# Attention and a two-layer network on one core: bursts of three chunks, A@V and three chunks, and another load of the first quad

## The chip, the cores and the metric

The kernel runs on one core of a Trainium2 chip. A core has five engines that run side by side, each through its own list of instructions in order: TensorE (PE in the profile, with PEld for the loading of weights), VectorE (DVE), ScalarE (ACT), GpSimd (POOL) and SyncE (SP). Semaphores order them against each other. TensorE reads on-chip memory (SBUF) and writes to PSUM, eight banks of 512 f32 values in each of 128 partitions; VectorE and ScalarE empty PSUM. Transfers between HBM and SBUF are issued from SP, ACT or POOL.

The metric is the device time of one execution in microseconds. Before the change it is 388.61 us, the median of three runs (388.48 to 388.9).

## The reference

Eight batches of 12 heads, 448 tokens, 64 dimensions per head. Each head's attention is a squared ReLU in place of a softmax, and its result feeds a network with 2048 hidden values:

```
scores = q @ k.T / sqrt(64)
attn   = max(scores, 0) ** 2 / 448
x      = attn @ v                       # heads side by side: 3584 tokens x 768
h      = x @ w_in                       # 768 -> 2048
g      = max(h, 0) + alpha * min(h, 0)
out    = g @ w_out                      # 2048 -> 768, float32
```

## The kernel before

Four heads of a batch make a *quad*; there are three quads per batch, 24 in all, numbered `n`. The 448 tokens are 64 times 7; a *chunk* `j` of 0 to 6 is one seventh of k's tokens for the four heads of a quad. So a quad has seven chunks.

Per quad there are these steps. **Loads**: `load_qk` and `load_v` bring q, k and v by POOL's queue, casting f32 to bf16 on the way. **Turning**: q and k are needed with the head dimension on partitions (tile `T`). For quads 0 to 5 `turn_pe` does it by transposes on PE (L153) and copies out of PSUM on DVE or ACT (L156); for later quads `turn_dma` has DVE rearrange them (L161) and SP issue a transposing DMA (L163). **Scores**: `score_mm` (L175) is one chunk, four matmuls of 64 x 64 weights on the four quarters of the array, which run side by side, into a pair of PSUM banks. **ReLU**: L184 on ACT or L186 on DVE, out of PSUM. **Square**: L194 on DVE or L192 on ACT. **A@V**: `attnv` (L204), 28 matmuls on quarters of the array, seven steps of four, into a pair of banks; the first bank is emptied by ACT (L214) and the second by DVE (L215) into `xT`.

Per batch there are then two stages that use the whole array. `f1` (L238) makes one of 16 blocks of 128 hidden values with six matmuls, and `f1_out` forms the leaky ReLU with ACT (L246) and DVE (L247) into `gT`. `f2` (L261) makes a block of 128 tokens by 384 output columns with 16 matmuls over `gT`; the copy out of PSUM is on ACT (L263) and two DMAs on SP write it (L269). Since `gT` covers two batches, six such blocks come behind an even batch and eight behind an odd one.

The order is written out by hand: the scheduler is off (`manual_schedule`), so every engine runs in the order of the program's lines. The attention of the next batch is laid between the blocks of the present one. In the loop over batches 2 to 7 the unit is `burst(n)`: three chunks of scores, A@V of quad n, two chunks, then all squares that are due. A *plain burst*, `run(some(3))`, is three chunks and their squares alone. Per batch there are two plain bursts, ahead of f1 blocks 6 and 12, and three bursts between output blocks, two output blocks apart (three in places). `prepare(n)` turns quad n by DMA and issues the loads of quad n + 2; it stands ahead of f1 blocks 1 and 9 and ahead of the second burst. Batches 0 and 1 are written out in single lines, since their attention has to be made before there is other work to lay it between.

PSUM is handed out in turn: `take_bank` gives the bank that was taken longest ago and `take_pair` the pair whose later bank was taken longest ago. Whoever gets a bank waits until what was in it has been read.

At the start q of quad 0 comes in f32 by SP's queue and the first four of its seven blocks of k by ACT's queue, both plain; DVE and ACT cast them. The last three blocks of k come by POOL's casting queue (L129). Transposes of those three stand behind three chunks of scores. 36 matmuls of an identity (L133) run meanwhile. POOL's queue goes on with q and k of quad 1, v of quad 0, q and k of quad 2, v of quads 1 and 2, and then the weights.

Of the kernel before, what the change touches and what calls it, by code (L numbers as in the profile page):

```python
# [10 lines left out]
F32 = mybir.dt.float32  # L11
BF16 = mybir.dt.bfloat16
# [4 lines left out]
NJ = 7  # L17
# [3 lines left out]
def kernel(  # L21
# [18 lines left out]
    HALF = d_model // 2  # L40
# [16 lines left out]
    ident = singles.tile([128, 128], BF16)  # L57
# [26 lines left out]
    def take_bank():  # L84
        i = min(range(8), key=lambda i: (taken[i], i))
        take(i, 1)
        return psum[:, i]


    raw, vraw = {}, {}  # L90

    def load_qk(n):
        b, g = divmod(n, NG)
        for name, src in (("q", q), ("k", k)):
            t = raw_pool.tile([128, 2, NJ, D], BF16, tag=name, name=f"{name}raw")
# [21 lines left out]
    def load_w_out(h):  # L117
        nc.gpsimd.dma_start(out=w_out_sb[:, h], in_=w_out_v[h])

    FIRST = 4  # L120
    first, flat0 = {}, {}
    for name, src, eng, hi in (("q", q, nc.sync, NJ), ("k", k, nc.scalar, FIRST)):
        first[name] = singles.tile([128, 2, hi * D], F32, name=f"{name}first")
        flat0[name] = src[0].rearrange("(m two) (pp j) d -> (two pp) m (j d)", two=2, j=NJ)[:, :2]
        eng.dma_start(out=first[name], in_=flat0[name][:, :, :hi * D])
        raw[(0, name)] = raw_pool.tile([128, 2, NJ, D], BF16, tag=name, name=f"{name}raw")
    nc.sync.dma_start(out=alpha_sb, in_=moe_alpha.rearrange("(kf p) -> p kf", p=128))
    make_identity(nc, ident)
    nc.gpsimd.dma_start(out=raw[(0, "k")][:, :, FIRST:].rearrange("p m j d -> p m (j d)"),  # L129
                        in_=flat0["k"][:, :, FIRST * D:])  # L130
    warm = psum[:, 7, :128]
    for _ in range(36):
        nc.tensor.matmul(warm, ident, ident, start=True, stop=True)  # L133
    for name, lo, hi, copy in (("q", 0, 4, nc.vector.tensor_copy), ("q", 4, NJ, nc.scalar.copy),
                               ("k", 0, 2, nc.vector.tensor_copy), ("k", 2, FIRST, nc.scalar.copy)):
        copy(raw[(0, name)][:, :, lo:hi].rearrange("p m j d -> p m (j d)"), first[name][:, :, D * lo:D * hi])  # L136
    load_qk(1)
    load_v(0)
    load_qk(2)
    load_v(1)  # L140
    load_v(2)


    T = {}

    def turn_pe(n, parts=(("q", 0, NJ, "D"), ("k", 0, NJ, "D"))):
        if n not in T:
            T[n] = T_pool.tile([128, 2, NJ, 128], BF16, tag="T", name="T")
        for name, lo, hi, eng in parts:
            ps = take_bank().bitcast(BF16)  # L150
            for j in range(lo, hi):
                for s in range(2):
                    nc.tensor.transpose(ps[64 * s:64 * s + 64, 128 * j:128 * j + 128], raw[(n, name)][:, s, j], ident)  # L153
            dst = T[n][:, "qk".index(name), lo:hi].rearrange("p j c -> p (j c)")
            copy = nc.vector.tensor_copy if eng == "D" else nc.scalar.copy
            copy(dst, ps[:, 128 * lo:128 * hi])  # L156

    def turn_dma(n):
        p = perm_pool.tile([128, 2, NJ, 2, D], BF16, tag="perm", name="perm")
# [21 lines left out]
    def relu(ps, eng):  # L181
        rl = rl_pool.tile([128, 2, S], BF16, tag="rl", name="rl")
        if eng == "A":
            nc.scalar.activation(rl, ps[:, :, :S], ACTF.Relu)  # L184
        else:
            nc.vector.tensor_scalar(rl, ps[:, :, :S], 0.0, None, ALU.max)  # L186
        return rl
# [31 lines left out]
    def sc(chunks):  # L219

        for n, j, eng in chunks:
            late.append((n, j, relu(score_mm(n, j), eng)))

    def sq(k=99, eng="D"):
        for g in late[:k]:
            square(*g, eng)
        del late[:k]

    def run(chunks):
        sc(chunks)  # L230
        sq()
# [21 lines left out]
        f1_mm(ps, b, ff, range(KM))  # L253
        f1_out(ps, b, ff)

    def f2(sb, c, hf, parts=((0, HALF),)):
        o = o_pool.tile([128, HALF], F32, tag="o", name="osb")
        for lo, hi in parts:
            ps = take_bank()[:, :hi - lo]
            for ff in range(KF):  # L260
                nc.tensor.matmul(ps, gT[sb][:, ff, bass.ts(c, 128)], w_out_sb[:, hf, ff, lo:hi],  # L261
                                 start=(ff == 0), stop=(ff == KF - 1))
            nc.scalar.copy(o[:, lo:hi], ps)  # L263
            for u in range(2):
                blk = 2 * c + u
                b, j = 2 * sb + blk // NJ, blk % NJ
                rows = out[b * S:(b + 1) * S].rearrange("(pp j) d -> j pp d", j=NJ)
                eng = nc.scalar if u and hi - lo < HALF else nc.sync
                eng.dma_start(out=rows[j][:, hf * HALF + lo:hf * HALF + hi], in_=o[64 * u:64 * u + 64, lo:hi])  # L269


    pat = "ADAAAAA"
# [1 line left out]
    def ch(n, lo, hi, p=pat):  # L274
        return [(n, j, p[j]) for j in range(lo, hi)]

    load_w_in(0)
    load_w_in(1)
    turn_pe(0, (("q", 0, 4, "D"), ("q", 4, NJ, "A"), ("k", 0, 2, "D"), ("k", 2, FIRST, "D")))
    sc(ch(0, 0, 3))  # L280
    turn_pe(0, (("k", FIRST, NJ, "D"),))
    sc(ch(0, 3, 4))
    sq(3)
    load_qk(3)
    sc(ch(0, 4, 6))
# [70 lines left out]
    f1s(0, 8, 9)  # L356
    ps = take_bank()[:, :S]
    f1_mm(ps, 0, 9, range(KM))
    turn_pe(4, (("q", 0, NJ, "A"), ("k", 0, NJ, "D")))
    f1_out(ps, 0, 9)  # L360
    load_qk(7)
    load_v(7)
    f1s(0, 10, 12)
    sc(ch(3, 6, 7) + ch(4, 0, 2, "AA"))
    f1s(0, 12, 16)
    f2(0, 0, 0)
    sc(ch(4, 2, 5, "AAADAAA"))
    attnv(3)
    sc(ch(4, 5, 7, "AAAAAAD"))
    turn_pe(5)  # L370
    sq(3)
    sq(2, "A")
    load_qk(8)
    load_v(8)
    f2(0, 1, 0)
    sc(ch(5, 0, 3))
    attnv(4)
    sc(ch(5, 3, 5, "AAAADAA"))
    sq(3)
    sq(2, "A")  # L380
    f2(0, 2, 0)
    sc(ch(5, 5, 7, "AAAAAAD"))
    sq(1, "A")
    sq(1)


    chunks = [(n, j) for n in range(2 * NG, NQ) for j in range(NJ)]
# [2 lines left out]
    def some(k):  # L390
        lo = at_c[0]
        at_c[0] = min(lo + k, len(chunks))
        return [(n, j, e) for (n, j), e in zip(chunks[lo:at_c[0]], "ADA")]

    def burst(n):

        sc(some(3))
        attnv(n)
        sc(some(2))
        sq()  # L400

    early = []
    for ff in range(4):
        ps = take_bank()[:, :S]
        f1_mm(ps, 1, ff, range(4))
        early.append(ps)
        if ff == 1:
            attnv(5)
    for ff in range(KF):
        if ff < 4:  # L410
# [15 lines left out]
    f2(0, 1, 1)  # L426
    run(some(3))
    f2(0, 2, 1)
    run(some(3))
    f2(0, 4, 0)  # L430
    burst(6)
    f2(0, 4, 1)
    f2(0, 5, 0)
    prepare(10)
    burst(7)
    f2(0, 5, 1)
    f2(0, 6, 0)
# [59 lines left out]
```

## Time and profile before

| What | Value |
|---|---|
| Time, median of three runs | 388.61 us |
| Time of the profiled execution | 388.61 us |
| Its span, first to last instruction | 386.8 us |
| PE busy | 377.8 us, 98% of the span |
| DVE, ACT, POOL busy | 69%, 53%, 17% |
| f2 matmuls (L261) | 912, 151.1 us |
| f1 matmuls (L238) | 768, 149.5 us |
| scores (L175) | 672, 45.5 us |
| A@V (L204) | 672, 37.6 us |
| Granted clock of PE | 1.00 |

Matmuls are pipelined, and the matmuls on quarters of the array run side by side, so busy time of PE is no measure of how well it is used; the start times of successive blocks are. A line of the timeline gives the start and the length in us, the engine, the line of the kernel, the operation, output and inputs, the number of instructions merged into the line, and, in brackets, how long the engine stood idle before and what ended that. A line of the chain gives shares of the span by the engine whose work, or whose wait, the end of the program hangs on.

### The profile page before, as it was taken

What the parts mean: (1) busy time and instruction counts of PE and PEld (TensorE: products, weight loads), DVE (VectorE), ACT (ScalarE), POOL (GpSimd) and SP (SyncE); (2) the same over time, 40 slices, a digit from 0 to 9 for tenths busy, and PEclk for the clock granted to TensorE, in tenths of its full rate; (3) what the DMA queues carried; (4) which work ended last, traced back from release to release, by engine and by line L of the source; (5) the groups of instructions that cost most, each with busy time, mean ns of one, the idle gap of its engine ahead of it and who ended that gap; (6) DMA issues with size and microseconds to landing.
All of it is one profiled execution on the core that took longest, in us unless ns stands there. A gap on an engine that the chain in (4) does not pass through costs nothing.

```text
span 386.8 us, 7918 instructions
## 1 busy us (share of the span) xinstructions
PE 377.8 (98%) x3228; PEld 211.1 (55%) x3228; DVE 266.0 (69%) x421; ACT 206.4 (53%) x332; POOL 64.0 (17%) x95
## 2 busy tenths in 40 slices
PE   7799999999999999999999999999999999999996
PEld 5444564555665456545555455654555545655564
DVE  4977876786868878789655896689754887626300
ACT  5977686355555664455445554547543475434311
POOL 8567211421022202022110221120000000000000
PEclk9999999999999999999999999999999999999999
DMA  9999999999393775687292871937025300120023
GB/s 163 187 204 204 204 213 216 157 188 197 79 151 73 115 134 82 122 140 114 47 175 51 138 120 42 176 53 140 22 68 99 74 0 23 42 61 2 14 70 82
DMA packets 71365, 42.97 MB, mean 111 GB/s; under 512 B 38432, under 2 KB 71328, under 8 KB 71328
## 3 DMA queue, kind: packets, MB, share of 16 engines
q0 software_dynamic: 26768, 22.45, 39.8%
q1 hardware_dynamic: 44128, 19.65, 24.0%
q8 instruction: 25, 0.41, 0.4%
q10 hardware_dynamic: 432, 0.36, 0.3%
q14 instruction: 12, 0.10, 0.1%
HBM read 45.62 MB, written 11.01 MB: 146 GB/s over the span
## 4 chain that ended last, share of the span: by engine, by line
PE 94%; DVE 3%; DMA 1%; ACT 1%; issue 0%; ACTq 0%
PE psum L238 38%; PE psum L261 38%; PE psum L175 9%; PE psum L204 8%; DMA qfirst<-in_q_dram 1%; DVE at L194 1%; PE psum L153 1%; DVE T L156 1%; ACT rl L184 1%; DVE rl L186 1%; ACT osb L263 0%; ACTq L269 0%; DVE qraw L136 0%; ACTq L184 0%; ACTq L263 0%
## 5 line engine op out<-in xcount | busy, mean ns | idle before, releaser
L261 PE MATMUL psum<-w_out_sb,gT 128*128 128x384 bf16 (+2 forms) x912 | 151.1, 323 | 0.0
L238 PE MATMUL psum<-xT,w_in_sb 128*128 128x448 bf16 x768 | 149.5, 353 | 0.4 <-ACT rl L184 0.4
L261 PEld LDWEIGHTS <-gT 128*128 128x128 bf16 x912 | 86.7, 98 | 63.0 <-issue 8.2
L238 PEld LDWEIGHTS <-w_in_sb 128*128 128x128 bf16 x768 | 73.7, 98 | 72.4 <-issue 5.6
L247 DVE SCALAR_TENSOR_TENSOR gT<-neg,beta_sb,psum 128x448 bf16<-128x448 f32 x128 | 83.2, 676 | 30.7 <-ACT neg L246 30.7
L246 ACT ACTIVATE neg<-psum 128x448 f32<-128x448 f32 x128 | 69.3, 547 | 64.0 <-PE psum L238 59.7
L184 ACT ACTIVATE rl<-psum 128x896 bf16<-128x896 f32 x112 | 97.2, 933 | 0.5 <-PE psum L175 0.5
L194 DVE TENSOR_TENSOR at<-rl 128x896 bf16<-128x896 bf16 x162 | 90.6, 616 | 0.0
L186 DVE TENSOR_SCALAR rl<-psum 128x896 bf16<-128x896 f32 x56 | 60.8, 1086 | 43.1 <-PE psum L175 43.1
L263 ACT COPY osb<-psum 128x384 f32<-128x384 f32 (+2 forms) x57 | 27.0, 474 | 105.3 <-PE psum L261 98.4
L175 PE MATMUL psum<-T 64*64 64x448 bf16 x672 | 45.5, 356 | 2.9 <-DVE T L156 1.4
L97 POOL DMA_DIRECT2D qraw<-in_q_dram x23 | 16.5, 718 | 172.0 <-DVE perm L161 162.8
L204 PE MATMUL psum<-at,vraw 64*64 64x448 bf16 x672 | 37.6, 351 | 0.3 <-DVE at L194 0.2
L204 PEld LDWEIGHTS <-vraw 64*64 64x64 bf16 x672 | 24.3, 106 | 11.0 <-issue 2.8
L175 PEld LDWEIGHTS <-T 64*64 64x64 bf16 x672 | 18.2, 105 | 21.5 <-issue 14.4
L215 DVE TENSOR_SCALAR xT<-psum 128x448 bf16<-128x448 f32 x23 | 14.4, 624 | 16.1 <-PE psum L204 11.7
L97 POOL DMA_DIRECT2D kraw<-in_k_dram x23 | 16.5, 717 | 14.0 <-DMA w_out_sb<-in_moe_w_out_dram 12.9
L104 POOL DMA_DIRECT2D vraw<-in_v_dram x24 | 17.2, 718 | 0.8 <-issue 0.3
L214 ACT ACTIVATE xT<-psum 128x448 bf16<-128x448 f32 x23 | 12.7, 551 | 3.2 <-PE psum L204 3.2
L161 DVE COPY perm<-qraw 128x896 bf16<-128x896 bf16 x18 | 11.0, 611 | 2.6 <-DMA T<-perm 2.6
L114 POOL DMA_DIRECT2D w_in_sb<-in_moe_w_in_dram x16 | 10.1, 629 | 7.6 <-DMA w_in_sb<-in_moe_w_in_dram 3.0
L161 DVE COPY perm<-kraw 128x896 bf16<-128x896 bf16 x18 | 10.9, 608 | 0.0
(24 smaller groups left out, 41.3 us busy)
## 6 DMA issues: line engine op xcount, KB each, us to landing
out_dram<-osb SPq DMA_DIRECT2D x110, 96.0 KB, 2.2
vraw<-in_v_dram POOLq DMA_DIRECT2D x24, 224.0 KB, 7.7
qraw<-in_q_dram POOLq DMA_DIRECT2D x23, 224.0 KB, 4.9
kraw<-in_k_dram POOLq DMA_DIRECT2D x23, 224.0 KB, 6.6
w_in_sb<-in_moe_w_in_dram POOLq DMA_DIRECT2D x16, 192.0 KB, 8.0
w_out_sb<-in_moe_w_out_dram POOLq DMA_DIRECT2D x2, 1536.0 KB, 18.6
qfirst<-in_q_dram SPq DMA_DIRECT2D x1, 448.0 KB, 4.3
T<-perm SPq DMA_TRANSPOSE x18, 6.9
```

The source lines that it names most:

```text
L97: nc.gpsimd.dma_start(out=t.rearrange("p m j d -> p m (j d)"), in_=flat[:, 2 * g:2 * g + 2])
L161: nc.vector.tensor_copy(p[:, i], raw.pop((n, name)).rearrange("p s j d -> p j s d"))
L175: nc.tensor.matmul(ps[64 * c:64 * c + 64, r, :S], t[64 * r:64 * r + 64, 1, j, 64 * c:64 * c + 64], t[64 * r:64 * r + 64, 0, :, 64 * c:64 * ...
L184: nc.scalar.activation(rl, ps[:, :, :S], ACTF.Relu)
L186: nc.vector.tensor_scalar(rl, ps[:, :, :S], 0.0, None, ALU.max)
L194: nc.vector.tensor_tensor(a, rl, rl, ALU.mult)
L204: nc.tensor.matmul(ps[64 * s:64 * s + 64, r, :S], vv[64 * r:64 * r + 64, s, j, :], a[64 * r:64 * r + 64, s], start=(j == 0), stop=(j == NJ ...
L238: nc.tensor.matmul(ps, w_in_sb[:, km // 2, km % 2, bass.ts(ff, 128)], xT[b][:, km // 2, km % 2, :], start=(km == 0), stop=(km == KM - 1))
L246: nc.scalar.activation(neg, ps, ACTF.Relu, scale=-1.0)
L247: nc.vector.scalar_tensor_tensor(gT[b // 2][:, ff, (b % 2) * S:(b % 2) * S + S], neg, beta_sb[:, ff:ff + 1], ps, ALU.mult, ALU.add)
L261: nc.tensor.matmul(ps, gT[sb][:, ff, bass.ts(c, 128)], w_out_sb[:, hf, ff, lo:hi], start=(ff == 0), stop=(ff == KF - 1))
L263: nc.scalar.copy(o[:, lo:hi], ps)
```

## The change

Six things change.

1. `burst(n)` has three chunks behind A@V in place of two, and squares five of its six chunks on DVE and one on ACT.
2. Per batch one plain burst is left, ahead of f1 block 6. The three `prepare` calls stand ahead of f1 blocks 1, 8 and 13, and none ahead of a burst (but for quad 10, whose place ahead of an output block is kept).
3. The copy of the last output block ahead of a burst is made by DVE in place of ACT (`eng="D"`).
4. In the last third of batch 0 and at the start of batch 1 the bursts are cut anew: the turn of quad 5 comes ahead of A@V 3, with one of its copies on ACT; the burst around A@V 3 has three chunks behind it (the last two of quad 4 and the first of quad 5), the one around A@V 4 has the other six of quad 5, so the burst of two chunks goes; two output blocks follow each other; A@V 5 comes one f1 block later.
5. Ahead of the first large burst there are three plain bursts in place of four.
6. At the start q and k of quad 0 both come whole in f32 by SP's and ACT's queues. DVE casts four blocks of q; ACT casts the other three and all of k. All transposes of quad 0 stand ahead of its first scores, and all four copies out of PSUM are DVE's. POOL's queue begins with v of quad 0, and then has q, k and v of quads 1 and 2.

```diff
-    FIRST = 4
-    first, flat0 = {}, {}
-    for name, src, eng, hi in (("q", q, nc.sync, NJ), ("k", k, nc.scalar, FIRST)):
...
+    first = {}
+    for name, src, eng in (("q", q, nc.sync), ("k", k, nc.scalar)):
+        first[name] = singles.tile([128, 2, NJ * D], F32, name=f"{name}first")
+        eng.dma_start(out=first[name], in_=src[0].rearrange("(m two) (pp j) d -> (two pp) m (j d)", two=2, j=NJ)[:, :2])
...
-    nc.gpsimd.dma_start(out=raw[(0, "k")][:, :, FIRST:].rearrange("p m j d -> p m (j d)"),
-                        in_=flat0["k"][:, :, FIRST * D:])
+    load_v(0)
...
-    for name, lo, hi, copy in (("q", 0, 4, nc.vector.tensor_copy), ("q", 4, NJ, nc.scalar.copy),
-                               ("k", 0, 2, nc.vector.tensor_copy), ("k", 2, FIRST, nc.scalar.copy)):
-        copy(raw[(0, name)][:, :, lo:hi].rearrange("p m j d -> p m (j d)"), first[name][:, :, D * lo:D * hi])
-    load_qk(1)
-    load_v(0)
-    load_qk(2)
-    load_v(1)
-    load_v(2)
+    for name, cut in (("q", ((0, 4, nc.vector.tensor_copy), (4, NJ, nc.scalar.copy))),
+                      ("k", ((0, 2, nc.scalar.copy), (2, NJ, nc.scalar.copy)))):
+        t = raw_pool.tile([128, 2, NJ, D], BF16, tag=name, name=f"{name}raw")
+        for lo, hi, copy in cut:
+            copy(t[:, :, lo:hi].rearrange("p m j d -> p m (j d)"), first[name][:, :, D * lo:D * hi])
+        raw[(0, name)] = t
+    for n in range(1, NG):
+        load_qk(n)
+        load_v(n)
...
-    def f2(sb, c, hf, parts=((0, HALF),)):
+    def f2(sb, c, hf, parts=((0, HALF),), eng="A"):
...
-            nc.scalar.copy(o[:, lo:hi], ps)
+            (nc.vector.tensor_copy if eng == "D" else nc.scalar.copy)(o[:, lo:hi], ps)
...
-    turn_pe(0, (("q", 0, 4, "D"), ("q", 4, NJ, "A"), ("k", 0, 2, "D"), ("k", 2, FIRST, "D")))
-    sc(ch(0, 0, 3))
-    turn_pe(0, (("k", FIRST, NJ, "D"),))
-    sc(ch(0, 3, 4))
+    turn_pe(0, ((0, 4, "D"), (4, NJ, "D")), ((0, 2, "D"), (2, NJ, "D")))
+    sc(ch(0, 0, 4))
     sq(3)
...
-    f2(0, 0, 0)
+    f2(0, 0, 0, eng="D")
+    turn_pe(5, ((0, NJ, "A"),))
     sc(ch(4, 2, 5, "AAADAAA"))
     attnv(3)
-    sc(ch(4, 5, 7, "AAAAAAD"))
-    turn_pe(5)
+    sc(ch(4, 5, 7, "AAAAAAD") + ch(5, 0, 1))
     sq(3)
-    sq(2, "A")
+    sq(1, "A")
+    sq()
     load_qk(8)
     load_v(8)
     f2(0, 1, 0)
-    sc(ch(5, 0, 3))
+    f2(0, 2, 0, eng="D")
+    sc(ch(5, 1, 4, "AADAAAA"))
     attnv(4)
-    sc(ch(5, 3, 5, "AAAADAA"))
+    sc(ch(5, 4, 7, "AAAAADA"))
     sq(3)
-    sq(2, "A")
-    f2(0, 2, 0)
-    sc(ch(5, 5, 7, "AAAAAAD"))
     sq(1, "A")
     sq(1)
+    sq(1, "A")
...
         sc(some(3))
         attnv(n)
-        sc(some(2))
-        sq()
+        sc(some(3))
+        sq(5)
+        sq(1, "A")
...
-        if ff == 1:
+        if ff == 2:
             attnv(5)
...
     f2(0, 2, 1)
-    run(some(3))
-    f2(0, 4, 0)
+    f2(0, 4, 0, eng="D")
     burst(6)
     f2(0, 4, 1)
-    f2(0, 5, 0)
     prepare(10)
+    f2(0, 5, 0, eng="D")
     burst(7)
     f2(0, 5, 1)
-    f2(0, 6, 0)
+    f2(0, 6, 0, eng="D")
     burst(8)
...
-            if not last and ff in (6, 12):
+            if not last and ff == 6:
                 run(some(3))
-            if not last and ff in (1, 9):
-                prepare(n0 + 2 + ff // 8)
+            if not last and ff in (1, 8, 13):
+                prepare(n0 + 2 + (1, 8, 13).index(ff))
...
-                g = at[i]
-                if g == 1:
-                    prepare(n0 + 4)
-                burst(n0 + g)
+                burst(n0 + at[i])
...
-                f2(*u)
+                f2(*u, eng="D" if i + 1 in at and not last else "A")
```

The function `turn_pe` is rewritten to take the cuts of q and of k apart; what it issues for a quad is 28 transposes and the copies out of PSUM, as before.

More of the change, by code (lines that the diff above doesn't have):

```diff
@@ L118, in load_w_out @@
         nc.gpsimd.dma_start(out=w_out_sb[:, h], in_=w_out_v[h])
-    FIRST = 4
-    first, flat0 = {}, {}
-    for name, src, eng, hi in (("q", q, nc.sync, NJ), ("k", k, nc.scalar, FIRST)):
[L123 to L126, printed above, removed]
+    first = {}
+    for name, src, eng in (("q", q, nc.sync), ("k", k, nc.scalar)):
+        first[name] = singles.tile([128, 2, NJ * D], F32, name=f"{name}first")
+        eng.dma_start(out=first[name], in_=src[0].rearrange("(m two) (pp j) d -> (two pp) m (j d)", two=2, j=NJ)[:, :2])
     nc.sync.dma_start(out=alpha_sb, in_=moe_alpha.rearrange("(kf p) -> p kf", p=128))
     make_identity(nc, ident)
-    nc.gpsimd.dma_start(out=raw[(0, "k")][:, :, FIRST:].rearrange("p m j d -> p m (j d)"),
-                        in_=flat0["k"][:, :, FIRST * D:])
+    load_v(0)
     warm = psum[:, 7, :128]
@@ L133 @@
         nc.tensor.matmul(warm, ident, ident, start=True, stop=True)
-    for name, lo, hi, copy in (("q", 0, 4, nc.vector.tensor_copy), ("q", 4, NJ, nc.scalar.copy),
-                               ("k", 0, 2, nc.vector.tensor_copy), ("k", 2, FIRST, nc.scalar.copy)):
-        copy(raw[(0, name)][:, :, lo:hi].rearrange("p m j d -> p m (j d)"), first[name][:, :, D * lo:D * hi])
-    load_qk(1)
-    load_v(0)
-    load_qk(2)
-    load_v(1)
-    load_v(2)
-    T = {}
[L146 to L156, printed above, removed]
+    for name, cut in (("q", ((0, 4, nc.vector.tensor_copy), (4, NJ, nc.scalar.copy))),
[4 more added lines that the diff above has]
+        raw[(0, name)] = t
@@ new lines, with turn_pe @@
+    for n in range(1, NG):
+        load_qk(n)
+        load_v(n)
+    T = {}
+    def turn_pe(n, cuts=((0, NJ, "D"),), cuts_k=((0, NJ, "D"),)):
+        t = T_pool.tile([128, 2, NJ, 128], BF16, tag="T", name="T")
+        for i, name in enumerate("qk"):
+            src = raw.pop((n, name))
+            for lo, hi, eng in (cuts, cuts_k)[i]:
+                ps = take_bank().bitcast(BF16)
+                for j in range(lo, hi):
+                    for s in range(2):
+                        nc.tensor.transpose(ps[64 * s:64 * s + 64, 128 * j:128 * j + 128], src[:, s, j], ident)
+                dst = t[:, i, lo:hi].rearrange("p j c -> p (j c)")
+                if eng == "D":
+                    nc.vector.tensor_copy(dst, ps[:, 128 * lo:128 * hi])
+                else:
+                    nc.scalar.copy(dst, ps[:, 128 * lo:128 * hi])
+        T[n] = t
@@ L267, in f2 @@
                 rows = out[b * S:(b + 1) * S].rearrange("(pp j) d -> j pp d", j=NJ)
-                eng = nc.scalar if u and hi - lo < HALF else nc.sync
-                eng.dma_start(out=rows[j][:, hf * HALF + lo:hf * HALF + hi], in_=o[64 * u:64 * u + 64, lo:hi])
+                queue = nc.scalar if u and hi - lo < HALF else nc.sync
+                queue.dma_start(out=rows[j][:, hf * HALF + lo:hf * HALF + hi], in_=o[64 * u:64 * u + 64, lo:hi])
     pat = "ADAAAAA"
@@ L358 @@
     f1_mm(ps, 0, 9, range(KM))
-    turn_pe(4, (("q", 0, NJ, "A"), ("k", 0, NJ, "D")))
+    turn_pe(4, ((0, NJ, "A"),))
     f1_out(ps, 0, 9)
```

## The prediction

> **What bounds the kernel now.** I read the page first: shares of busy time, then the chain that ended last.
>
> ```profile
> PE 377.8 (98%) x3228; PEld 211.1 (55%) x3228; DVE 266.0 (69%) x421; ACT 206.4 (53%) x332; POOL 64.0 (17%) x95
> PE 94%; DVE 3%; DMA 1%; ACT 1%; issue 0%; ACTq 0%
> ```
>
> PE is the bound, and from about 21 us on the chain is nothing but PE work. So a change to this kernel counts in three ways only: what PE pays when it changes between kinds of matmul, any new wait of PE, and the start. The PE timeline of one batch prices the first.
>
> ```profile
> 162.56 6.97 PE L238 MATMUL psum<-xT,w_in_sb 128*128 128x448 bf16 x36
> 169.46 0.76 PE L175 MATMUL psum<-T 64*64 64x448 bf16 x12
> 170.15 6.98 PE L238 MATMUL psum<-xT,w_in_sb 128*128 128x448 bf16 x36
> 177.07 0.76 PE L175 MATMUL psum<-T 64*64 64x448 bf16 x12
> 177.76 4.71 PE L238 MATMUL psum<-xT,w_in_sb 128*128 128x448 bf16 x24
> 182.31 2.76 PE L261 MATMUL psum<-w_out_sb,gT 128*128 128x384 bf16 x16
> 185.01 0.76 PE L175 MATMUL psum<-T 64*64 64x448 bf16 x12
> 185.64 1.52 PE L204 MATMUL psum<-at,vraw 64*64 64x448 bf16 x28
> 186.97 0.57 PE L175 MATMUL psum<-T 64*64 64x448 bf16 x8
> ```
>
> Start to start, 24 full-array matmuls before other full-array ones take 182.31 - 177.76 = 4.55 us, 0.19 each; 36 would be 6.83. Before scores, 36 take 169.46 - 162.56 = 6.90: 0.08 more. Three chunks of scores are twelve matmuls, four at a time on quarters of the array, so three passes of 0.19 = 0.57; they take 170.15 - 169.46 = 0.69, 0.12 more. **One visit to the small tiles thus costs 0.20 us** beyond its work. Inside a burst A@V takes 186.97 - 185.64 = 1.33, seven passes of 0.19: no visible charge.
>
> The same timeline with ACT and DVE shows what a burst waits for.
>
> ```profile
> 141.95 0.76 PE L175 MATMUL psum<-T 64*64 64x448 bf16 x12
> 142.06 0.48 ACT L263 COPY osb<-psum 128x384 f32<-128x384 f32 x1 [2.06 <-PE psum L261]
> 142.59 1.52 PE L204 MATMUL psum<-at,vraw 64*64 64x448 bf16 x28
> 143.91 0.57 PE L175 MATMUL psum<-T 64*64 64x448 bf16 x8
> 144.14 0.54 ACT L214 ACTIVATE xT<-psum 128x448 bf16<-128x448 f32 x1
> ```
>
> Call the first score's start S (141.95). The copy of the last output block ends at S + 0.59, and A@V, which here takes that block's bank as its first, starts 0.05 later, at S + 0.64. Where that bank is A@V's second (S = 106.67) it starts at S + 0.59 and its matmuls are drawn out by 0.04. The whole burst takes 2.46 either way, and 2.51 where the copy ended 0.05 later (98.86). So A@V already hangs on that copy, and what the copy loses, the burst loses.
>
> **The change, part by part** (lines are those of before).
>
> *Fewer visits.* The order of PE's program gives seven fewer: one in batch 1 (chunks 5 and 6 of quad 5 join a burst), one plain burst fewer ahead of the first large burst, one fewer in each of batches 2 to 6. The matmuls are the same 3228. 7 x 0.20 = **-1.4 us**.
>
> *The copy ahead of a burst on DVE.* The trace has no f32 copy from PSUM on DVE. Nearest rows: L186 reads 896 f32 in 1.086 us and L215 448 in 0.624, 1.03 ns per element, so 384 take 0.624 - 0.066 = 0.56. Lower end: the L156 copy of 384 bf16, 0.35; upper end: the 0.624 itself. I take 0.56, since the L186 and L215 rows read the same f32. DVE is free at S (the five squares end over a microsecond earlier: two output blocks, 5.3 us, lie between bursts) and would start at S + 0.11 to 0.15, as ACT and DVE do after PE in the rows above. It ends near S + 0.69 in place of S + 0.59, so 0.09 more per burst. The banks handed out by `take_bank` and `take_pair` in turn put that block's bank into A@V's pair in 18 bursts: 18 x 0.09 = **+1.6**. At 0.35 the wait goes (18 x -0.05 = -0.9), at 0.624 it is +2.8. ACT gains nothing from it: its first relu waits for the first chunk (0.44 after S at the start of the program, 0.49 in the burst above).
>
> [...]
>
> *Three chunks behind A@V.* Five chunks used three pairs of banks before A@V and A@V's own, then two more; the next output block found a bank that a relu had long emptied. With six, the oldest bank left is A@V's first, which ACT empties (L214). In the rows above that evacuation starts 144.14 - 143.91 = 0.23 after A@V's successor, takes 0.54, and PE follows 0.05 later: 0.82. PE is through three chunks and the way back in 0.69. In the bursts with the block in the second bank the figures are 0.20 + 0.55 + 0.05 = 0.80 against 0.73. So 0.07 to 0.13, 0.09 on average, in all 19 bursts of this form: **+1.7**. Bounds: nothing, if PE's way back hides it, and 19 x 0.13 = 2.5.
>
> [...]
>
> *Quad 0.* q and k now both come whole in f32 by the SP and ACT queues, so k's last three blocks, 98 KB as bf16 on POOL's queue, become 196 KB of f32. The windows view has 404 GB/s from 3.5 to 4 us, and 40 from 4.5 to 5, when the plain loads are nearly through and casting ones begin. At 400 the extra lands in 0.5 us; sharing half and half with casting loads, in 1.0. I take 0.7: q at about 5.75 in place of 5.04, k at 5.95. Then one chain: ACT casts the rest of q and k in turn (0.51, 0.40, and about 0.74 for 640 columns, from 0.40 at 256 and 0.51 at 384; each starts some 0.1 before its forerunner ends) to 7.24, the transposes of k follow, and because all of them stand ahead of the first score, it starts near 7.6, not 6.70.
>
> ```profile
> 5.06 0.51 ACT L136 CAST qraw<-qfirst 128x384 bf16<-128x384 f32 x1 [2.50 <-DMA qfirst<-in_q_dram]
> 6.70 0.76 PE L175 MATMUL psum<-T 64*64 64x448 bf16 x12 [0.28 <-DVE T L156]
> 7.14 7.39 ACT L184 ACTIVATE rl<-psum 128x896 bf16<-128x896 f32 x9 [0.49 <-PE psum L175]
> ```
>
> From that first relu ACT is busy without a gap to 23 us (2.00 of each 2.00 us in the windows from 8 to 22), and its instructions there are the same in both kernels. So the whole delay reaches PE's steady stage: **+0.9**, between 0.5 and 1.6. `load_v(0)` now runs ahead of quad 1's loads on POOL: they land about 1 us later (8.16 and 9.27 before), as late as PE comes to them. The weights slip by some 0.5 us: half 0 of `w_out` landed at 43.96 for a use at 45.82, which itself slips.
>
> *Batch 1.* The transposes of quad 5 move ahead of a burst, with one copy on ACT: its relus and L214 run later, about 0.1 more of the wait above. A@V 5 follows its last scores by twelve matmuls, 2.3 us, with three squares on DVE behind a relu, two on ACT: relus end near S + 4.6, the sixth square near S + 6.4, and A@V reaches it at S + 6.2. **+0.3** together, 0 to 0.8.
>
> *At no cost.* The third `turn_dma` of a batch moves from a burst to f1 block 13, the second from 9 to 8: each two DVE copies (0.61), three loads on POOL, a transpose on SP. A block gives PE 1.14 us and DVE 0.68 (L247), so the 1.1 us of copies is recovered in three blocks; the last gT is read 2.4 us after f1 ends. Without that slack the first f2 block would wait up to 0.7 per batch. T is used a batch later, against 6.9 us to landing; SP's outputs gain, since a transpose leaves their stretch. One square per burst on ACT (0.95) ends before its next copy is due.
>
> Sum: -1.4 + 1.6 + 1.7 + 0.9 + 0.3 = **+3.1 us**. The profiled execution took 388.61 (span 386.8 and 1.8 around it), which is the median too: **391.7 us**, 0.8% slower.
>
> **Rivals.**
> *Only the counts matter.* The waits view has no wait of PE after 24 us, so both burst waits may stay hidden in the changes between tile sizes: 388.6 - 1.4 + 0.9 + 0.3 = 388.4. Against it: the 0.05 by which A@V follows the copy in every burst of the one kind.
> *DVE copies f32 at the bf16 row's rate* (not slower). Place: the copy at each of 18 bursts. At 0.35 us A@V no longer waits and the term is -0.9: +0.6, 389.2, no difference that can be told. It decides below about 0.43 us per copy. For it only the L156 rows; against it L186 and L215.
> *No wait behind the burst:* L214 ends in time. +1.4, 390.0.
> *A late start as well:* k lands at 6.6 and the start costs 1.6: 392.4.
>
> **How the numbers follow.** This kernel's measurement tells 0.2%, 0.8 us, from no change: 387.8 to 389.4. Chances: forecast 0.50, only counts 0.15, fast copy 0.13, no wait behind 0.12, late start 0.10. Only counts and fast copy spread over the bound below: 0.12 faster, 0.16 same, the rest slower, 0.72. The likeliest with its bounds is 390.6 to 393.0; the range down to the first two rivals is 387.9 to 392.9.
>
> **What would show it.** In the profile after: seven fewer visits in PE's timeline; the DVE copy at 0.56 us and A@V at S + 0.70 or later; the first f2 block 0.80 after A@V's successor, not 0.69; a burst of 2.8 us rather than 2.65 (2.46 plus one pass); the first relu near 8.0 us. I am wrong if the copy is much shorter, if f2 starts at 0.70 all the same, or if the first relu stays near 7.2.

## The result, and the profile after

The changed kernel takes 390.19 us in the median of six runs (389.71 to 390.79), the kernel before 388.59 in the same session (388.48 to 388.99): a ratio of 1.004, interval 1.0027 to 1.0053. It is slower, as forecast, by 1.6 us where 3.1 was forecast. The profiled execution took 390.4 us (span 388.6), 1.8 more than that of before.

The page of the changed kernel: busy time of PE, the shares of the chain by engine, and the group of the moved copies.

```profile
PE 378.4 (97%) x3228; PEld 214.5 (55%) x3228; DVE 262.7 (68%) x418; ACT 219.9 (57%) x334; POOL 63.2 (16%) x94
PE 93%; DVE 3%; ACT 2%; DMA 1%; issue 0%; ACTq 0%
L264 DVE COPY osb<-psum 128x384 f32<-128x384 f32 x20 | 11.2, 558 | 40.4 <-PE psum L262 40.4
```

The matmuls are the same 3228. The copy on DVE takes 0.558 us; 0.56 was derived. ACT has 2% of the chain in place of 1%: the page now lists ACT's emptying of A@V's bank (L215; L214 before) with 1% of the chain, and did not list it before.

The PE timeline of the batch whose rows of before stand in the prediction (lines are those of the changed kernel: L239 f1, L262 f2, L176 scores, L205 A@V):

```profile
163.46 6.97 PE L239 MATMUL psum<-xT,w_in_sb 128*128 128x448 bf16 x36
170.36 0.76 PE L176 MATMUL psum<-T 64*64 64x448 bf16 x12
171.06 11.52 PE L239 MATMUL psum<-xT,w_in_sb 128*128 128x448 bf16 x60
182.42 2.76 PE L262 MATMUL psum<-w_out_sb,gT 128*128 128x384 bf16 x16
185.11 0.76 PE L176 MATMUL psum<-T 64*64 64x448 bf16 x12
185.83 1.52 PE L205 MATMUL psum<-at,vraw 64*64 64x448 bf16 x28
187.15 0.76 PE L176 MATMUL psum<-T 64*64 64x448 bf16 x12
187.97 7.96 PE L262 MATMUL psum<-w_out_sb,gT 128*128 128x384 bf16 x48
```

The visit before f1 block 12 is gone. Before, 36 and 24 f1 matmuls with the visit between took 182.31 - 170.15 = 12.16; now 60 take 182.42 - 171.06 = 11.36. Of the 0.80 saved, three chunks (0.57) moved into bursts, so the visit was worth 0.23 (0.20 was forecast). But scores to A@V is 185.83 - 185.11 = 0.72 (0.64 before), and A@V's successor to the output block 187.97 - 187.15 = 0.82 for three chunks.

Bursts come in two kinds, by the place of the last block's bank in A@V's pair. S is again the start of a burst's first score, and a burst lasts from S to the start of the block behind it. A burst of the first kind, that bank first, with DVE and ACT:

```profile
141.93 0.76 PE L176 MATMUL psum<-T 64*64 64x448 bf16 x12
142.04 0.56 DVE L264 COPY osb<-psum 128x384 f32<-128x384 f32 x1 [1.34 <-PE psum L262]
142.65 1.52 PE L205 MATMUL psum<-at,vraw 64*64 64x448 bf16 x28
143.97 0.76 PE L176 MATMUL psum<-T 64*64 64x448 bf16 x12
144.20 0.54 ACT L215 ACTIVATE xT<-psum 128x448 bf16<-128x448 f32 x1
144.79 0.49 PE L262 MATMUL psum<-w_out_sb,gT 128*128 128x384 bf16 x2
```

The copy ends at 142.60 and A@V starts 0.05 later, at S + 0.72; the emptying of A@V's first bank ends at 144.74 and the output block starts 0.05 later. The burst takes 0.72 + 1.32 + 0.82 = 2.86. The other kind, bank second:

```profile
106.91 0.76 PE L176 MATMUL psum<-T 64*64 64x448 bf16 x12
107.01 0.56 DVE L264 COPY osb<-psum 128x384 f32<-128x384 f32 x1 [0.52 <-PE psum L262]
107.50 1.64 PE L205 MATMUL psum<-at,vraw 64*64 64x448 bf16 x28
108.82 0.88 PE L176 MATMUL psum<-T 64*64 64x448 bf16 x12
109.03 0.55 ACT L215 ACTIVATE xT<-psum 128x448 bf16<-128x448 f32 x1
109.64 0.66 PE L262 MATMUL psum<-w_out_sb,gT 128*128 128x384 bf16 x3
```

Here it is 0.59 + 1.32 + 0.82 = 2.73. The copy's delay shows only in A@V being drawn out (1.64, not 1.52), and the next scores too (0.88, not 0.76). Of the 20 copies on DVE 18 stand ahead of such bursts, nine of each kind. Without any wait six chunks would take 2.46 + 0.19 = 2.65, an estimate from the burst of before and one pass of four matmuls, so the first kind loses 0.21 and the second 0.08. The forecast had charged 0.22 and 0.16.

The start:

```profile
5.41 0.68 DVE L134 CAST qraw<-qfirst 128x512 bf16<-128x512 f32 x1 [5.41 <-DMA qfirst<-in_q_dram]
7.55 0.99 PE L176 MATMUL psum<-T 64*64 64x448 bf16 x16 [0.17 <-DVE T L154]
7.98 1.73 ACT L185 ACTIVATE rl<-psum 128x896 bf16<-128x896 f32 x2 [1.13 <-PE psum L176]
25.40 3.20 PE L239 MATMUL psum<-xT,w_in_sb 128*128 128x448 bf16 x16
```

The last of these lines has this counterpart in the profile of before:

```profile
24.74 3.20 PE L238 MATMUL psum<-xT,w_in_sb 128*128 128x448 bf16 x16
```

q is first read at 5.41 (before 5.06), the first relu starts at 7.98 (before 7.14). But PE's steady stage, the first run of 16 f1 matmuls, starts at 25.40 in place of 24.74: 0.66 late, not 0.84.

### The profile page after: what moved, and what is told of

It is laid out like the page before. It is cut to its first block, busy times and chain, and to the rows that moved or that the text cites. A ratio compares the mean times of both kernels' runs of the same rounds, so it can differ in the third digit from the quotient of the medians.

```text
span 388.6 us, 7937 instructions
## 1 busy us (share of the span) xinstructions
PE 378.4 (97%) x3228; PEld 214.5 (55%) x3228; DVE 262.7 (68%) x418; ACT 219.9 (57%) x334; POOL 63.2 (16%) x94
## 4 chain that ended last, share of the span: by engine, by line
PE 93%; DVE 3%; ACT 2%; DMA 1%; issue 0%; ACTq 0%
PE psum L262 38%; PE psum L239 38%; PE psum L205 9%; PE psum L176 7%; ACT xT L215 1%; DMA qfirst<-in_q_dram 1%; DVE at L195 1%; PE psum L151 1%; DVE T L154 1%; DVE rl L187 1%; ACT rl L185 1%; DVE qraw L134 0%; ACT osb L264 0%; ACTq L270 0%; ACTq L264 0%
## 5 line engine op out<-in xcount | busy, mean ns | idle before, releaser
L262 PE MATMUL psum<-w_out_sb,gT 128*128 128x384 bf16 (+2 forms) x912 | 150.6, 323 | 0.5
L239 PE MATMUL psum<-xT,w_in_sb 128*128 128x448 bf16 x768 | 148.7, 353 | 0.4 <-ACT rl L185 0.4
L185 ACT ACTIVATE rl<-psum 128x896 bf16<-128x896 f32 x118 | 101.3, 932 | 44.8 <-PE psum L176 44.8
L262 PEld LDWEIGHTS <-gT 128*128 128x128 bf16 x912 | 87.6, 98 | 63.1 <-issue 7.9
L239 PEld LDWEIGHTS <-w_in_sb 128*128 128x128 bf16 x768 | 74.1, 98 | 71.6 <-issue 4.2
L195 DVE TENSOR_TENSOR at<-rl 128x896 bf16<-128x896 bf16 x147 | 82.1, 617 | 0.0
L187 DVE TENSOR_SCALAR rl<-psum 128x896 bf16<-128x896 f32 x50 | 54.3, 1086 | 3.9 <-PE psum L176 3.8
L176 PE MATMUL psum<-T 64*64 64x448 bf16 x672 | 45.3, 355 | 2.6 <-ACT rl L185 1.0
L264 ACT COPY osb<-psum 128x384 f32<-128x384 f32 (+2 forms) x37 | 17.4, 472 | 40.3 <-PE psum L262 38.5
L264 DVE COPY osb<-psum 128x384 f32<-128x384 f32 x20 | 11.2, 558 | 40.4 <-PE psum L262 40.4
L205 PE MATMUL psum<-at,vraw 64*64 64x448 bf16 x672 | 37.8, 351 | 0.5 <-ACT rl L185 0.2
L176 PEld LDWEIGHTS <-T 64*64 64x64 bf16 x672 | 20.6, 106 | 19.3 <-issue 12.6
L205 PEld LDWEIGHTS <-vraw 64*64 64x64 bf16 x672 | 24.5, 106 | 11.8 <-issue 5.7
L193 ACT ACTIVATE at<-rl 128x896 bf16<-128x896 bf16 x21 | 20.1, 963 | 0.5
L215 ACT ACTIVATE xT<-psum 128x448 bf16<-128x448 f32 x23 | 12.7, 552 | 6.1 <-PE psum L205 5.0
```

The lines of the kernel that those rows point to most:

```text
L176: nc.tensor.matmul(ps[64 * c:64 * c + 64, r, :S], t[64 * r:64 * r + 64, 1, j, 64 * c:64 * c + 64], t[64 * r:64 * r + 64, 0, :, 64 * c:64 * ...
L193: nc.scalar.activation(a, rl, ACTF.Square)
L195: nc.vector.tensor_tensor(a, rl, rl, ALU.mult)
L205: nc.tensor.matmul(ps[64 * s:64 * s + 64, r, :S], vv[64 * r:64 * r + 64, s, j, :], a[64 * r:64 * r + 64, s], start=(j == 0), stop=(j == NJ ...
L239: nc.tensor.matmul(ps, w_in_sb[:, km // 2, km % 2, bass.ts(ff, 128)], xT[b][:, km // 2, km % 2, :], start=(km == 0), stop=(km == KM - 1))
L264: (nc.vector.tensor_copy if eng == "D" else nc.scalar.copy)(o[:, lo:hi], ps)
```

## The experiments

Each run's ratio is to the kernel before, timed in the same session; its median was 388.59, 388.60 and 388.69 us in the three sessions. In the result two theories were left for the bursts of the second kind, which lost half of what the forecast had charged. One, W: PE always waits behind the burst for the emptying of A@V's first bank, and where the bank is second that wait hides the copy's delay. The other, L: only the late copy makes the bursts long.

**Output copies back on ACT.**

```diff
-            (nc.vector.tensor_copy if eng == "D" else nc.scalar.copy)(o[:, lo:hi], ps)
+            nc.scalar.copy(o[:, lo:hi], ps)
```

> The kernel after, with every output copy on ACT again. S is the start of a burst's first score. In the profile after, 9 bursts take 2.86 us (the output block's bank is A@V's first) and 9 take 2.73 (it is A@V's second); 2.65 would be free of waits. Both theories: in the first kind A@V starts at S + 0.64 in place of 0.72, 9 x 0.08 = 0.7 us less. Theory W (behind a burst PE waits for ACT's emptying of A@V's first bank, in both kinds): the second kind stays at 2.72, the first goes to 2.78; time 390.2 - 0.7 = 389.5. Theory L (in the second kind it is only the copy's lag on the second bank's matmuls that is carried to the end of the burst): the second kind falls to 2.65; time 390.2 - 1.4 = 388.8.

Measured: 389.05 us (388.71 to 389.37), ratio 1.001 (1.0001 to 1.0019). Timeline of the first kind:

```profile
141.71 0.76 PE L176 MATMUL psum<-T 64*64 64x448 bf16 x12
141.82 0.48 ACT L264 COPY osb<-psum 128x384 f32<-128x384 f32 x1 [2.06 <-PE psum L262]
142.35 1.52 PE L205 MATMUL psum<-at,vraw 64*64 64x448 bf16 x28
143.67 0.77 PE L176 MATMUL psum<-T 64*64 64x448 bf16 x12
143.90 0.54 ACT L215 ACTIVATE xT<-psum 128x448 bf16<-128x448 f32 x1
144.49 1.30 PE L262 MATMUL psum<-w_out_sb,gT 128*128 128x384 bf16 x7
```

The second kind:

```profile
106.74 0.76 PE L176 MATMUL psum<-T 64*64 64x448 bf16 x12
108.66 0.80 PE L176 MATMUL psum<-T 64*64 64x448 bf16 x12
108.86 0.54 ACT L215 ACTIVATE xT<-psum 128x448 bf16<-128x448 f32 x1
109.46 0.81 PE L262 MATMUL psum<-w_out_sb,gT 128*128 128x384 bf16 x4
```

In the first kind A@V is back at S + 0.64, and yet the output block still comes 0.82 after A@V's successor, 0.05 after L215 ends. Bursts take 2.78 and 2.72 (one, the first of the first trio, a trio being the three bursts of one batch, 2.75): against the changed kernel the first kind is shorter by 0.08, the second by 0.01. L, which wanted 2.65 for the second kind, is out. There the copy's move costs next to nothing, since the wait behind the burst is there with or without it.

**The last block's bank always second.** A@V takes the same pair, but writes the half that was taken earlier first, and ACT empties that one.

```diff
-        ps = take_pair()
+        first, ps = take_pair_older_first()
...
-                    nc.tensor.matmul(ps[64 * s:64 * s + 64, r, :S],
+                    nc.tensor.matmul(ps[64 * s:64 * s + 64, r ^ first, :S],
...
```

> The kernel after, with A@V writing first into that bank of its pair that was taken earlier, so that the last output block's bank is always the second. Same work, same copies on DVE. The theory that the place of the bank decides (a late copy costs where the bank is first, and is covered where it is second): the 9 bursts of 2.86 go to 2.73, time 390.2 - 1.2 = 389.0. The forecast's theory (0.09 wherever in the pair the bank lies): no change, 390.2.

Measured: 388.73 us (388.48 to 389.1), ratio 1.0001 (0.9992 to 1.001). All 18 bursts take 2.73. The order of two banks is worth 9 x 0.13 = 1.2 us. The two profiled executions differ by 1.6, and the other 0.4 of it is the start, which varies (below): the steady f1 starts at 24.93 here, 0.47 earlier. In the medians the gain is 1.46.

**The start of before in the changed kernel.** The diff's lines on quad 0 undone, all else kept; its core:

```diff
-    turn_pe(0, ((0, 4, "D"), (4, NJ, "D")), ((0, 2, "D"), (2, NJ, "D")))
-    sc(ch(0, 0, 4))
+    turn_pe(0, (("q", 0, 4, "D"), ("q", 4, NJ, "A"), ("k", 0, 2, "D"), ("k", 2, FIRST, "D")))
+    sc(ch(0, 0, 3))
+    turn_pe(0, (("k", FIRST, NJ, "D"),))
+    sc(ch(0, 3, 4))
```

> The kernel after with the start of the kernel before (four blocks of k plain, three by the casting queue, transposes of the last three behind three chunks). The first relu back at 7.1 us from 8.0. Theory that the delay of the start is carried through ACT's full queue to PE's steady stage, less what A@V 2 gains: 390.2 - 0.7 = 389.5; by the forecast's term of 0.9: 389.3. Rival, that the delay is lost in later waits: 390.2.

Measured: 390.05 us (389.67 to 390.21), ratio 1.0034 (1.0022 to 1.0047). In the profiled execution the steady f1 starts at 24.64 and the time is 0.73 less than in that of the changed kernel; in the median the gain is 0.14. One execution is no measure of this start.

**The copy on DVE alone, in the kernel before.**

```diff
-                f2(*u)
+                f2(*u, eng="D" if i + 1 in at and not last else "A")
```

and the same in the written-out blocks ahead of the first three large bursts.

> The kernel before with nothing changed but the copy of the last output block ahead of a burst, on DVE. Two chunks behind A@V, so PE does not wait for A@V's bank there: the cost of the copy by itself. 9 of these bursts have the block in A@V's first bank, 8 in its second. Forecast's theory, 0.09 each: 388.6 + 1.5 = 390.1, all bursts near 2.55. Theory that only the first kind pays: 388.6 + 0.7 = 389.3, the second kind stays at 2.46. Theory L (the lag is carried out of the burst where nothing else covers it): like the forecast, the second kind at 2.54.

Measured: 392.7 us (392.45 to 392.86), ratio 1.0104 (1.009 to 1.0118): +4.1, far outside the expectation. With two chunks behind A@V most bursts of both kinds rise by 0.08, from 2.46 to 2.54 or 2.55 (the three that already took 2.51 rise by 0.04): where nothing waits behind the burst, the copy costs the second kind as much as the first. But the middle burst of each of five trios takes 3.09. Its timeline (lines of before; L161 are the copies of `prepare`):

```profile
107.03 0.56 DVE L263 COPY osb<-psum 128x384 f32<-128x384 f32 x1 [1.39 <-PE psum L261]
107.51 0.61 DVE L161 COPY perm<-qraw 128x896 bf16<-128x896 bf16 x1
108.03 0.61 DVE L161 COPY perm<-kraw 128x896 bf16<-128x896 bf16 x1
108.56 1.08 DVE L186 TENSOR_SCALAR rl<-psum 128x896 bf16<-128x896 f32 x1
109.70 0.38 PE L175 MATMUL psum<-T 64*64 64x448 bf16 x4 [0.35 <-DVE rl L186]
```

`prepare` stands between the copy and the burst. With the copy on ACT its two DVE copies ran while PE was in the output block; with the copy on DVE they queue behind it, since it cannot start before that block ends, and the relu of the second chunk starts 1.0 us late. PE waits for that relu's banks.

**The same with `prepare` moved ahead of that output block.**

```diff
-                if g == 1:
-                    prepare(n0 + 4)
...
+            if at.get(i + 1) == 1 and not last:
+                prepare(n0 + 4)
```

> The kernel before with the copy ahead of a burst on DVE and the second burst's prepare moved ahead of the output block before it. If the 0.55 us in every trio's second burst came from the two rearranging copies that queue between the copy and the relu on DVE, these bursts fall from 3.09 to 2.54, and only 17 x 0.08 = 1.4 is left: 390.0 us. If the copy itself delays them, the time stays at 392.7.

Measured: 390.31 us (390.27 to 390.52), ratio 1.0045 (1.0032 to 1.0058). Four of the five bursts fall to 2.54 or 2.55; the fifth, in the written-out trio of batch 1, kept its `prepare` where it was, and its 3.09. One of the four, of the second kind:

```profile
150.45 0.76 PE L175 MATMUL psum<-T 64*64 64x448 bf16 x12
151.04 1.64 PE L204 MATMUL psum<-at,vraw 64*64 64x448 bf16 x28
152.37 0.69 PE L175 MATMUL psum<-T 64*64 64x448 bf16 x8
152.99 0.50 PE L261 MATMUL psum<-w_out_sb,gT 128*128 128x384 bf16 x2
```

A@V starts at S + 0.59 and is drawn out to 1.64, as in the changed kernel, but here the delay reaches the output block. So the two copies queued behind the output copy did make the 0.55. The bursts' own lengths give 13 x 0.08, 3 x 0.04 and one 0.63, together 1.8; without the 0.55 of the `prepare` that stayed, the copy alone costs about 1.2 us in this kernel.

**Quad 0 alone, in the kernel before.** The diff's lines on the start in the kernel before, and nothing else; its core:

```diff
-    turn_pe(0, (("q", 0, 4, "D"), ("q", 4, NJ, "A"), ("k", 0, 2, "D"), ("k", 2, FIRST, "D")))
-    sc(ch(0, 0, 3))
-    turn_pe(0, (("k", FIRST, NJ, "D"),))
-    sc(ch(0, 3, 4))
+    turn_pe(0, ((0, 4, "D"), (4, NJ, "D")), ((0, 2, "D"), (2, NJ, "D")))
+    sc(ch(0, 0, 4))
```

> The kernel before with the changed kernel's quad 0 and nothing else: q and k whole in f32, all transposes ahead of the first scores, v of quad 0 first on POOL's queue. The forecast's term is +0.9, so 389.5 us. The two profiles (steady f1 at 25.40 in place of 24.74) say +0.66, 389.25. The run with the start of before in the changed kernel gained 0.14 in the median, which says 388.7. If the start differs from execution to execution more than from kernel to kernel, the scatter of the runs is wider than the 0.4 us of before and the profile's steady f1 lies between 24.7 and 25.4.

Measured: 389.11 us (388.9 to 389.45), ratio 1.0012 (1.0003 to 1.0021): +0.5. In its profiled execution:

```profile
5.04 0.51 ACT L134 CAST qraw<-qfirst 128x384 bf16<-128x384 f32 x1 [2.48 <-DMA qfirst<-in_q_dram]
7.58 1.73 ACT L185 ACTIVATE rl<-psum 128x896 bf16<-128x896 f32 x2 [1.09 <-PE psum L176]
```

q lands at 5.04, no later than before, and still the first relu is 0.44 late: the casts and transposes that now all stand ahead of the first scores. The steady f1 starts at 25.00, 0.26 late.

**The emptying of A@V's pair swapped**, DVE the first bank and ACT the second, in the changed kernel.

```diff
-        nc.scalar.activation(xT[b][:, g, 0], ps[:, 0, :S], ACTF.Copy, scale=out_scale)
-        nc.vector.tensor_scalar(xT[b][:, g, 1], ps[:, 1, :S], out_scale, None, ALU.mult)
+        nc.scalar.activation(xT[b][:, g, 1], ps[:, 1, :S], ACTF.Copy, scale=out_scale)
+        nc.vector.tensor_scalar(xT[b][:, g, 0], ps[:, 0, :S], out_scale, None, ALU.mult)
```

> The changed kernel with A@V's first bank emptied by DVE (0.62 us, starting 0.27 after A@V's successor) and the second by ACT, in place of the reverse (0.54, starting 0.20 to 0.23). If the block behind a burst hangs on the emptying of the first bank, it starts 0.27 + 0.62 + 0.05 = 0.94 after A@V's successor in place of 0.81, bursts take 2.98 and 2.85, and 19 of them add 2.3 to 2.5 us: 392.6. If it hangs on something else, such as the change of tile size or the weights of the block, bursts stay at 2.86 and 2.73 and the time at 390.2.

Measured: 391.64 us (391.58 to 391.97), ratio 1.0081 (1.0067 to 1.0095). A burst of the first kind:

```profile
143.96 0.76 PE L176 MATMUL psum<-T 64*64 64x448 bf16 x12
144.18 0.63 DVE L216 TENSOR_SCALAR xT<-psum 128x448 bf16<-128x448 f32 x1 [0.55 <-PE psum L205]
144.22 0.55 ACT L215 ACTIVATE xT<-psum 128x448 bf16<-128x448 f32 x1
144.86 1.46 PE L262 MATMUL psum<-w_out_sb,gT 128*128 128x384 bf16 x8
```

The output block again starts 0.05 after the engine that empties the first bank is done, now DVE, and no longer follows ACT, which ended 0.04 earlier. Bursts take 2.94 and 2.87. The 2.94 is less than the 2.98 expected, since DVE starts 0.22 after A@V's successor here, not 0.27: in this kind the emptying of the first bank starts 0.04 before that of the second, whichever engine has it (144.18 and 144.22 here, 144.20 and 144.24 in the changed kernel). In the second kind, 2.85 expected, DVE starts 0.28 after it.

**Each bank emptied by both engines**, ACT the first 240 columns and DVE the other 208 (with the two edits of the first experiments).

```diff
-        nc.scalar.activation(xT[b][:, g, 0], ps[:, first, :S], ACTF.Copy, scale=out_scale)
-        nc.vector.tensor_scalar(xT[b][:, g, 1], ps[:, 1 - first, :S], out_scale, None, ALU.mult)
+        for r in (first, 1 - first):
+            nc.scalar.activation(xT[b][:, g, int(r != first), :CUT], ps[:, r, :CUT], ACTF.Copy, scale=out_scale)
+            nc.vector.tensor_scalar(xT[b][:, g, int(r != first), CUT:], ps[:, r, CUT:S], out_scale, None, ALU.mult)
```

> The changed kernel with all output copies on ACT, the last block's bank always second in A@V's pair, and each bank of A@V emptied by both engines at once, ACT the first 240 columns and DVE the other 208. By the rows ACT needs about 0.34 us and DVE 0.38, so the block behind the burst can start 0.65 to 0.70 after A@V's successor. If the emptying of the first bank is what PE waits for, all bursts fall from 2.72 to 2.65 and 18 x 0.07 = 1.3 goes: 387.3 us, below before. If two engines on one bank slow each other, or the block hangs on something else, bursts stay at 2.72 or more and the time at 388.6 or above.

Measured: 393.66 us (393.53 to 394.09), ratio 1.0132 (1.0118 to 1.0146). The timeline:

```profile
109.81 0.80 PE L183 MATMUL psum<-T 64*64 64x448 bf16 x12
110.01 0.63 ACT L225 ACTIVATE xT<-psum 128x240 bf16<-128x240 f32 x2
110.42 0.65 DVE L226 TENSOR_SCALAR xT<-psum 128x208 bf16<-128x208 f32 x2 [0.81 <-ACT xT L225]
110.84 1.46 PE L272 MATMUL psum<-w_out_sb,gT 128*128 128x384 bf16 x8 [0.24 <-DVE xT L226]
```

The two engines did not work at once: DVE stands idle until ACT's part of the same bank is done, and follows it. DVE's first part ends near 110.80 and the block starts at 110.84. So the question whether two engines on one bank slow each other is not answered; what the run shows is that an emptying that ends later moves PE by as much. Bursts take 2.95.

**Second bank and copies on ACT together; the same with the start of before.** The edits are those shown above, put together:

```diff
-        ps = take_pair()
+        first, ps = take_pair_older_first()
...
-            (nc.vector.tensor_copy if eng == "D" else nc.scalar.copy)(o[:, lo:hi], ps)
+            nc.scalar.copy(o[:, lo:hi], ps)
...
```

> The changed kernel with two edits of earlier runs together: the last block's bank always second in A@V's pair, and all output copies on ACT. If what is left in second-bank bursts is the emptying of A@V's first bank alone, all 18 take 2.72, no better than with the copy on DVE: body of 363.7 behind a steady f1 at 24.9 to 25.2, 388.6 to 388.9 us. If the copy still costs its 0.08 there, they fall to 2.65 and the time to 387.4.

> The same two edits and the start of before. If the changed start costs 0.3 (the mean of the steady f1 in the runs so far, 25.07 against 24.74) it is 0.3 below the run without it: 388.3 to 388.6 us, 0 to 0.3 below before. By the forecast's 0.9 it would be 387.8.

Measured: 388.46 us (388.17 to 389.49), ratio 0.9998 (0.9989 to 1.0007); and 388.16 us (387.98 to 388.56), ratio 0.9987 (0.9978 to 0.9995). All bursts but the first of the first trio (2.75) take 2.72 in both: with the bank second, DVE's copy and ACT's differ by 0.01 per burst (0.03 from one burst's start to the next, since the block behind it is shorter too: 8.03 us with DVE, 8.01 with ACT). The start is worth 0.3 here. The second is the only version whose interval lies below 1. It gains 0.13% on the kernel before, less than the 0.2% that the prediction took as what a measurement of this kernel can tell.

**A@V in columns 64 to 511, the part that the output block overwrites emptied first.** This is built on the last version, with its start of before.

```diff
+        OFF = 64 if n else 0
...
-                    nc.tensor.matmul(ps[64 * s:64 * s + 64, r ^ first, :S],
+                    nc.tensor.matmul(ps[64 * s:64 * s + 64, r ^ first, OFF:OFF + S],
...
-        nc.scalar.activation(xT[b][:, g, 0], ps[:, first, :S], ACTF.Copy, scale=out_scale)
+        cut = HALF - OFF
+        for lo, hi in ((0, cut), (cut, S)):
+            nc.scalar.activation(xT[b][:, g, 0, lo:hi], ps[:, first, OFF + lo:OFF + hi], ACTF.Copy, scale=out_scale)
...
```

> As the run before, but A@V writes columns 64 to 511 of its banks and ACT empties columns 64 to 383 of the first bank ahead of 384 to 511, since the block behind the burst writes columns 0 to 383 alone. By the rows 320 columns take ACT 0.42 us in place of 0.54. If PE waits for this emptying and for those columns alone, the block follows A@V's successor by 0.20 + 0.42 + 0.05 = 0.67, PE's own way is 0.69, bursts fall from 2.72 to 2.65 and 18 x 0.07 = 1.3 goes: 387.0 to 387.3 us, 0.3 to 0.4% below before. If PE waits for the whole bank, the second part adds about 0.16 and bursts take 2.85: 390.5. If it is the change of tile size that takes 0.80, nothing changes: 388.4.

Measured: 389.41 us (389.01 to 389.52), ratio 1.0016 (1.0007 to 1.0025).

```profile
143.48 0.80 PE L182 MATMUL psum<-T 64*64 64x448 bf16 x12
143.68 0.60 ACT L225 ACTIVATE xT<-psum 128x320 bf16<-128x320 f32 x2
144.34 2.92 PE L272 MATMUL psum<-w_out_sb,gT 128*128 128x384 bf16 x17
```

The block starts at 144.34, 0.06 after the end of both parts (144.28), and does not follow the first, which by the 0.42 us that the rows of ACT give for 320 columns ended near 144.10, an estimate: in this program the wait is for the whole bank. Two parts take 0.60 in place of 0.54, and bursts 2.78 in place of 2.72, the same 0.06.

## Why the prediction was right in sign and twice as large as the change

Measured from the two profiled executions, whose times differ by 1.8 us:

| Term | Forecast | Measured |
|---|---|---|
| Seven visits fewer | -1.4 | -1.6: 5 x 0.23 and 2 x 0.22 |
| Copy ahead of a burst on DVE | +1.6 | +0.8: 9 x 0.08 + 9 x 0.01 |
| Three chunks behind A@V | +1.7 | +1.9: 10 x 0.13 + 9 x 0.07 |
| Quad 0 | +0.9 | +0.66; some 0.3 over all runs |
| Batch 1 beyond its waits | +0.3 | +0.2 |
| Three bursts of before that were 0.04 longer already (98.86, 205.75, 297.11), and blocks behind first-bank bursts 0.01 shorter | none | -0.25: 3 x 0.044 + 9 x 0.013 |
| End of the last output blocks | none | +0.1 |

These add to 1.8, as the two times have it.

*Right, and shown by runs.* The visits: removed, and at the price read from the timeline. The copy's duration, 0.558 us. The wait behind the burst: 0.13 and 0.07 were read from rows of before in which nothing waited, and the first two runs, and the swapped and the split emptying, show PE following the end of the first bank's emptying by 0.04 to 0.07 in every form. So "only the counts matter", "no wait behind" and "the fast copy" fell, and so did "a late start as well": k was being cast by 5.92 in every execution with this start, not read first at 6.6. "No wait behind" came nearest by its number alone (390.0 against 390.19). That is chance, since the wait that it denies cost 1.9 us. One thing stays argued: no run made this emptying end early enough to set PE free, and the two that were to do so, the split emptying and the one in two parts, made it end later.

*Where it failed: the step "18 x 0.09 = +1.6".* It charged the copy's delay in all 18 bursts ("what the copy loses, the burst loses") and then added the wait behind the burst in full. In a first-bank burst both are paid, since A@V as a whole starts 0.08 later (S + 0.72, not S + 0.64) and its end moves with it. In a second-bank burst A@V's first bank starts on time (S + 0.59) and is done on time (its emptying starts at S + 2.12 with the copy on either engine: 109.03 - 106.91, and 108.86 - 106.74 with ACT); the delay lies in the second bank alone, and PE's way to the output block, longer by 0.08 (the scores behind A@V take 0.88, and 0.80 with the copy on ACT), ends when the emptying of the first bank would have let it start anyhow. The two costs run beside each other and the larger counts. The copy alone costs 0.08 in both kinds (the two runs on the kernel before), beside the wait only 0.01 (the copies back on ACT). So the term measured +0.8 in place of +1.6. Three smaller slips: the delay of a copy that ends at S + 0.69 and not S + 0.59 is 0.10 and not 0.09, and it measured 0.08; the average wait of 0.09, between 0.07 and 0.13, holds if two bursts in three are second-bank, and half of them are, so that the wait cost 1.9 and not 1.7; and three bursts of before were already 0.04 longer, which the sum left out.

*Mis-sized: the start, +0.9.* Two of its steps were wrong. q was put at 5.75; it was first read between 4.97 and 5.50 in seven executions with this start. And "the whole delay reaches PE's steady stage" was wrong: from the first relu to the steady f1 it is 17.60 us with the start of before (7.14 to 24.74) and 17.42 with the new one (7.98 to 25.40; 7.58 to 25.00), the same to 0.02 in every profile in which that stretch was left as it is, but for one (17.53). The 0.18 goes at A@V 2, which takes 1.45 in place of 1.63. That DVE no longer has a copy of k's transposes behind the first relu would explain it, but no run tried that alone. The start's cost in the median is 0.5, 0.3 and 0.14 us in the three pairs of kernels that differ in it alone; on the mean some 0.3, and it isn't settled closer.

*Right, but only for this program: "at no cost".* The moved `prepare` cost nothing, as forecast (the 60 f1 matmuls around it take 11.36 us, 0.189 each, as ever), and there is a reason for its place that the forecast had not seen: left ahead of the second burst it queues between the copy on DVE and the relu, which cost 5 x 0.55 us in the kernel before with that copy (the changed kernel was not run so). Quad 10's is one of the five. The diff moves it too, from directly ahead of the second burst to ahead of the output block in front of it, so its place is not kept, though the description of the change says so. The forecast asked what a moved step delays where it arrives, not what it would have delayed where it stood.

## What to carry to other kernels

Two delays on one path add only if the second begins where the first ends. Before summing waits at the two ends of a stage, ask for each kind of that stage whether the late thing also shifts the event that the next wait hangs on; where it does not, take the larger. And when a stage takes all buffers of a ring, look for the one that it gives back last: here the order of two banks within a pair, which costs nothing to choose, was worth 1.2 us of the 1.6 that the change lost.

## What had not been expected of the chip

The first transfer's landing differs between executions: q's first rows were read at 4.97, 5.01, 5.03, 5.04, 5.30, 5.41 and 5.50 us in executions with the same opening instructions, and the cast of 512 columns on DVE that follows took 0.43 us in five of them and 0.62 to 0.68 in those at 5.41 and 5.50 (0.43 to 0.58 in the six with the start of before, read from 4.82 to 5.06). PE's steady stage began between 24.81 and 25.98 us, while bursts of the same form kept their length to 0.01 us from one profile to the next. These are profiles of different kernels with one opening, one each, so that the runs of a single kernel differ mainly through the start is likely and not shown. A single profile prices a burst well and a start badly.
